# Expert blocks: the second 128 tokens' layer 2 put last and under a condition, second-layer weights split behind layer 1, block table made over three blocks

## The chip, the cores and the metric

The kernel runs on one NeuronCore of a Trainium2 chip. The metric is the device time of one execution in microseconds (us). Times of single instructions come from the hardware profiler's record of one execution. Engines are called as in the profile: PE is TensorE's matmul, PEld its weight load, DVE is VectorE, ACT ScalarE, POOL GpSimd, SP SyncE. A name with q (PEldq, POOLq) is that engine's sequencer, which handles branches, register loads and semaphore instructions.

## The reference, cut to what matters

Three stages follow each other: a linear-attention recurrence over 4 x 8 x 768 steps, a dense squared-ReLU layer pair (384 to 2048 to 384), and a routed expert layer. The change touches the third alone:

```
do_compute = x @ w_skip > 0                     # 3072 tokens of 384
e_idx = argmax(xc @ w_gate)                     # 8 experts
for e in range(8):
    mask = e_idx == e
    h = maximum(xc[mask] @ w1[e], 0)            # 384 -> 1024
    y[mask] = gate_w[mask] * (h @ w2[e])        # 1024 -> 384
out = x;  out[do_compute] = xc + y
```

Evaluated on the inputs, the reference sends 2397 of the 3072 tokens to experts 0 to 7 in numbers of 1155, 132, 435, 318, 112, 43, 143 and 59. Of expert 0's, 1064 stand in the first 2816 tokens.

## The kernel before, in words

The expert stage works in blocks of 256 tokens of one expert. Blocks 0 and 1 take the first 512 tokens of expert 0 while the dense stage's last tokens are still being routed; blocks 2 to 8 take the first 256 tokens of experts 1 to 7. What is left is listed in a table made at run time (`table`, lines 826 to 877): with the counts above these are three more blocks of expert 0 and one more each of experts 2 and 3, so that blocks 9 to 13 run and the 14 blocks of the profile are complete. Blocks from 9 on stand in nested conditions on the number of blocks `nblk` (`rest`, lines 974 to 978).

A block (`block`, lines 886 to 924) has eight slices `f` of 128 hidden units. Every product of float32 numbers is three matmuls, high by high, high by low, low by high. `l1(f)` is 9 matmuls of 256 columns into one of four PSUM banks; ACT then writes the high part `hh` (relu) and DVE the low part `hl`. `l2(f)` is, for each half `t` of 128 tokens, 3 matmuls of 384 columns that add to `acc[t]`; it follows `l1` by LAG = 4 slices. The last four slices' `l2` stand behind all of `l1`, first for half 0 and then for half 1. `finish(n, t)` (DVE, line 786) scales and adds the token row, `scatter(n, t)` (POOL, line 790, an indirect DMA) writes the rows out. A block always computes all 256 rows; rows without a token have an index outside the output.

Each block carries side work at times written out by hand in `CTP` (lines 73 to 77), in units of half a step: `gather(n + 2)` (POOL, line 772), `xprep(n + 1, t)` (three PE transposes at line 779, an ACT cast, a DVE subtraction), and for the next expert's weights eight pieces `ew_split`: ACT writes the high part (line 647), then DVE or POOL, as `CTP["e"]` says, the low part (line 648). Pieces 0 to 3 are `w1`, pieces 4 to 7 `w2`. Right behind the split of a piece, SP issues the load of the set after next into the freed buffer (line 637). The order on each engine is the program's order; semaphores between engines come from the tile framework. `nblk` and the register values for SP are read by `values_load`. The condition of line 729 jumps over the whole fallback for badly scaled inputs; it isn't taken here.

In the built program of this kernel a condition has a true arm and a false arm. [...]

Of the kernel before, what the change touches and what calls it, by code (L numbers as in the profile page):

```python
# [7 lines left out]
F32 = mybir.dt.float32  # L8
F32R = mybir.dt.float32r
BF16 = mybir.dt.bfloat16  # L10
I32 = mybir.dt.int32
# [60 lines left out]

CTP = {
    "l": [0.3, 1.2, 2.1, 2.6, 3.3, 4.1, 4.6, 5.7],
    "e": [0, 1, 0, 1, 0, 0, 1, 0],
    "x": [5.1, 5.6],
    "g": 2.6}
NX = NTOK // UT
NST = NE + 1
# [4 lines left out]
def rwkv_moe_kernel(ctx: ExitStack, tc: tile.TileContext, a_in, v_in, ud, wio,  # L84
# [659 lines left out]
    xgs = [[cp.tile([128, DM], F32, name=f"xg0_{t}") for t in range(2)]]  # L744
    ptx = [ptk, pu]
    xhs, xls = list(xth), list(xtl)
    exr, sct = {}, [None]

    def wset(n):

# [2 lines left out]
    def ids(n, t):  # L753
        if n < 2:
            l = lsp[0][:, 2 * n + t]
        elif n < NST:
            l = lsb[:, (n - 1) * LB + t]
        else:
            l = idt[:, n - NST, t]
        return l[:, 0:1], l[:, 1:2].bitcast(F32)  # L760
# [9 lines left out]
    def gather(n):  # L770
        for t in range(2):
            nc.gpsimd.indirect_dma_start(  # L772
                xgs[n % 4][t], None, x2d[:, :], bass.IndirectOffsetOnAxis(ap=ids(n, t)[0], axis=0),
                bounds_check=NTOK + PADR - 1, oob_is_err=False)

    def xprep(n, t):
        bank = ptx[t]
        for kc in range(KC):
            nc.tensor.transpose(bank[:, kc * 128:(kc + 1) * 128], xgs[n % 4][t][:, kc * 128:(kc + 1) * 128], ident)  # L779
        s = slice(t * 128, t * 128 + 128)  # L780
        src = bank[:, 0:DM].rearrange("p (k t) -> p k t", k=KC)
        nc.scalar.copy(xhs[n % 3][:, :, s], src)
        nc.vector.tensor_tensor(xls[n % 3][:, :, s], src, xhs[n % 3][:, :, s].bitcast(F32), ALU.subtract)

    def finish(n, t):
        nc.vector.scalar_tensor_tensor(yos[n % 2][t], acc[t][:, 0:DM], ids(n, t)[1], xgs[n % 4][t], ALU.mult, ALU.add)

    def scatter(n, t):

        i = nc.gpsimd.indirect_dma_start(  # L790
            out[:, :], bass.IndirectOffsetOnAxis(ap=ids(n, t)[0], axis=0), yos[n % 2][t], None,
            bounds_check=NTOK - 1, oob_is_err=False)
        if t:
            tc.declare_no_dep(i.ins, sct[0].ins, reason="rows of the other half of the block")
        sct[0] = i
# [11 lines left out]
    cq = ctx.enter_context(tc.tile_pool(name="cq", bufs=1, side="right"))  # L807
    ew_alloc(cq, 1)
    raws.append(cq.tile([128, 8, 768], F32, name="raw1"))
    xgs += [[cq.tile([128, DM], F32, name=f"xg{i}_{t}") for t in range(2)] for i in range(1, 4)]  # L810
    xhs.append(cq.tile([128, KC, UT], F32R, name="cxh2"))
    xls.append(cq.tile([128, KC, UT], F32R, name="cxl2"))
    yos = [[cq.tile([128, DM], F32, name=f"yo{i}_{t}") for t in range(2)] for i in range(2)]
    hps = pgs + [[cq.tile([128, UT], F32R, name=f"{n}{i}") for n in ("gh", "gl")] for i in range(NPB, LAG + 1)]
    ls2 = cq.tile([128, NE * LB, 2], I32, name="ls2")
    idt = cq.tile([128, NX, 2, 2], I32, name="idt")
    tx = cq.tile([1, 4, NE], F32, name="tx")
    ti = cq.tile([1, 2, NE], I32, name="ti")
    tm = cq.tile([1, 2, NX, NE], F32, name="tm")
    tv = cq.tile([1, 5, NX], F32, name="tv")  # L820
    tbl = cq.tile([1, 2, NX], I32, name="tbl")
    nbk = cq.tile([1, 1], I32, name="nbk")
    l1b = [ph[0], ph[1], pat.rearrange("p a b c -> p (a b c)"), py.rearrange("p a b -> p (a b)")]

    def table():


        V = nc.vector
        c0, f = cn0[0:1, 0:1], tx[:, 0, 0:1]
        ex, cx, g = tx[:, 1], tx[:, 2], tx[:, 3, 0:1]  # L830
        ind, pr = tm[:, 0], tm[:, 1]
        eb, sb, kb, z, bs = (tv[:, n] for n in range(5))
        on = cfs[0:1, 256:256 + NX]
        each = lambda a: a.unsqueeze(1).to_broadcast([1, NX, NE])

        def t1():
            V.tensor_tensor(f, c0, cnt[0:1, 0:1], ALU.is_lt)
            V.scalar_tensor_tensor(f, c0, float(2 * UT), f, ALU.is_lt, ALU.mult)
            V.tensor_scalar(ti[:, 0], cnt[0:1], 1, None, ALU.subtract)
            V.tensor_scalar(ti[:, 1], ti[:, 0], 8, None, ALU.arith_shift_right)  # L840

        def t2():

            V.tensor_scalar(ex, ti[:, 1], 0.0, None, ALU.max)  # L844
            V.tensor_scalar(g, f, 2.0, -1.0, ALU.mult, ALU.add)
            V.tensor_tensor(ex[:, 0:1], ti[:, 1, 0:1], g, ALU.add)
            V.tensor_scalar(ex[:, 0:1], ex[:, 0:1], 0.0, None, ALU.max)

        def t3():
            V.tensor_tensor_scan(cx, cfs[0:1, 256:256 + NE], ex, 0.0, ALU.mult, ALU.add)  # L850
            V.tensor_copy(nbk, cx[:, NE - 1:NE])
            V.tensor_tensor_scan(bs, on, on, -1.0, ALU.mult, ALU.add)

        def t4():
            V.tensor_tensor(ind, each(cx), bs.unsqueeze(2).to_broadcast([1, NX, NE]), ALU.is_le)
            V.tensor_tensor(pr, ind, each(ex), ALU.mult)
            V.tensor_reduce(eb, ind, AX.X, ALU.add)

        def t5():
            V.tensor_scalar(eb, eb, float(NE - 1), None, ALU.min)  # L860
            V.tensor_reduce(sb, pr, AX.X, ALU.add)
            V.tensor_tensor(kb, bs, sb, ALU.subtract)
            V.tensor_scalar(kb, kb, 1.0, None, ALU.add)

        def t6():

            V.tensor_scalar(z, eb, 0.0, g, ALU.is_equal, ALU.mult)
            V.tensor_tensor(kb, kb, z, ALU.subtract)
            V.tensor_scalar(kb, kb, 2.0, None, ALU.mult)

        def t7():
            V.scalar_tensor_tensor(kb, eb, float(LB), kb, ALU.mult, ALU.add)
            V.tensor_scalar(kb, kb, float(NE * LB - 2), None, ALU.min)
            V.tensor_copy(tbl[:, 0], eb)
            V.tensor_copy(tbl[:, 1], kb)

        return [(0.9 + m, f) for m, f in enumerate((t1, t2, t3, t4, t5, t6, t7))]

    def ex_load(b):
        exr[b] = nc.values_load(tbl[0:1, 0, b:b + 1], engines=[mybir.EngineType.SP], min_val=0, max_val=NE - 1)  # L880

    def id_load(b):
        c = nc.values_load(tbl[0:1, 1, b:b + 1], engines=[mybir.EngineType.SP], min_val=0, max_val=NE * LB - 2)
# [2 lines left out]
    def block(n, side):  # L886

        w1h, w1l, w2h, w2l = ew[wset(n) % 2]
        xh, xl = xhs[n % 3], xls[n % 3]

        def l1(f):
            h = l1b[f % 4][:, 0:UT]
            m = 0
            for w, xx in ((w1h, xh), (w1l, xh), (w1h, xl)):
                for kc in range(KC):
                    nc.tensor.matmul(h, w[:, kc, f * 128:(f + 1) * 128], xx[:, kc, :],  # L896
                                     start=(m == 0), stop=(m == 3 * KC - 1))
                    m += 1
            hh, hl = hps[f % (LAG + 1)]
            nc.scalar.activation(hh, h, AF.Relu)  # L900
            nc.vector.scalar_tensor_tensor(hl, h, 0.0, hh.bitcast(F32), ALU.max, ALU.subtract)  # L901

        def l2(f, ts=(0, 1)):
            hh, hl = hps[f % (LAG + 1)]
            for t in ts:
                s = slice(t * 128, t * 128 + 128)
                for m, (a, w) in enumerate(((hh, w2h), (hh, w2l), (hl, w2h))):
                    nc.tensor.matmul(acc[t][:, 0:DM], a[:, s], w[:, f, :],  # L908
                                     start=(f == 0 and m == 0), stop=(f == NJE - 1 and m == 2))

        steps = []
        for f in range(NJE):
            steps.append(lambda f=f: l1(f))
            if f >= LAG:
                steps.append(lambda f=f - LAG: l2(f))
        for t in range(2):
            for f in range(NJE - LAG, NJE, 2):
                steps.append(lambda f=f, t=t: (l2(f, (t,)), l2(f + 1, (t,))))
            steps.append(lambda t=t: (finish(n, t), scatter(n, t)))
        todo = sorted((v, m) for m, (v, _) in enumerate(side))  # L920
        for m, f in enumerate(steps):
            f()
            while todo and todo[0][0] < (m + 1) / 2:
                side[todo.pop(0)[1]][1]()

    def sides(n):
        side, last = [], NST + NX - 1

        def add(v, f):
            side.append((v, f))  # L930
# [3 lines left out]
        if n < last:  # L934
            for t in range(2):
                add(CTP["x"][t], lambda t=t: xprep(n + 1, t))
        w = wset(n) + 1
        if n and n < last:
            for p in range(8):
                add(CTP["l"][p], lambda p=p: ew_split(w, p, nc.gpsimd if CTP["e"][p] else nc.vector))  # L940
        if n and wset(n) + 3 <= last - 1:
# [2 lines left out]
                add(0.01, lambda: ex_load(q - NE))  # L944
            for p in range(8):
                add(CTP["l"][p] + 0.02, lambda p=p: ew_load(q, p, exr[q - NE] if q >= NE else None))
        if 3 <= n < 6:
            for b in range(4 * n - 12, 4 * n - 8):
                add(7 + 0.1 * (b % 4), lambda b=b: id_load(b))
        return side  # L950

# [15 lines left out]
    r2b()  # L967
    gather(1)
    block(0, side)
    for n in range(1, NST):  # L970
        block(n, sides(n) + (table() if n == 2 else []))
    nblk = nc.values_load(nbk[0:1, 0:1], min_val=0, max_val=NX)

    def rest(n):
# [83 lines left out]
```

## Time and profile before

| | |
|---|---|
| median of 3 runs | 910.76 us (910.37 to 911.51) |
| the profiled execution's own time | 911.02 us |
| its span, first to last instruction | 909.2 us |
| PE busy | 833.6 us (92%) |
| DVE busy | 611.6 us (67%) |
| POOL busy | 583.7 us (64%) |
| ACT busy | 495.7 us (55%) |
| expert blocks, first matmul to last | 645.8 to 893.8 us |
| the last block (13), first matmul | 876.17 us |

The profile gives for each engine the time in which it had an instruction running. Busy shares are means over stages with different limits, so what a change in the expert stage is worth is read from the stretch of that stage, from 646 us on.

### The profile page before, as it was taken

Reading aid. Unit: us, or ns where it says so; the run is one execution under the profiler, and the core shown is the slowest. Engines: PE = TensorE matmul, PEld = TensorE weight load, DVE = VectorE, ACT = ScalarE, POOL = GpSimd, SP = SyncE. Lnnn points to the kernel's source line nnn. Section 1 sums busy time; section 2 is a strip of 40 time slices with the busy share of each in tenths; the row PEclk is TensorE's granted clock in tenths of the full one; section 3 lists DMA queues with packets and bytes.
Section 4 is the critical chain, followed back from the end, with each engine's and each line's share of the span. In section 5 each row is a group of like instructions: output and inputs, shape, how many; then the busy total and the mean of one; then the engine's idle time right before and its main releaser. Section 6 shows DMA issues by size and latency. Waiting matters only on the chain. (4 is left out here: it accounts for less than half of the span.)

```text
span 909.2 us, 18684 instructions
## 1 busy us (share of the span) xinstructions
PE 833.6 (92%) x6790; PEld 792.0 (87%) x6790; DVE 611.6 (67%) x1273; ACT 495.7 (55%) x1229; POOL 583.7 (64%) x618
## 2 busy tenths in 40 slices
PE   2665799999999999999999999989999999999993
PEld 2544698999999999999999999979999999999993
DVE  7987962658585758575767676513468787777773
ACT  1343555666656565656565656647345554554551
POOL 8766976776777767676767676526355655554561
PEclk9955899999999999999999999989999999999997
DMA  8454322232222322222231311025486676567663
GB/s 209 139 182 116 131 61 52 78 78 78 52 78 52 77 56 75 63 68 74 56 87 43 87 44 56 2 93 194 147 304 203 212 237 221 186 218 236 211 208 115
DMA packets 67806, 110.92 MB, mean 122 GB/s; under 512 B 34452, under 2 KB 43944, under 8 KB 67696
## 3 DMA queue, kind: packets, MB, share of 16 engines
q1 hardware_dynamic: 60192, 97.46, 36.0%
q0 software_dynamic: 4736, 10.40, 3.5%
q10 hardware_dynamic: 2768, 1.69, 0.8%
q8 instruction: 57, 0.93, 0.4%
q14 instruction: 53, 0.43, 0.2%
HBM read 92.84 MB, written 16.15 MB: 120 GB/s over the span
## 5 line engine op out<-in xcount | busy, mean ns | idle before, releaser
L369 POOL TENSOR_TENSOR gl<-g,gh 128x256 fp32r<-128x256 f32 x192 | 150.0, 783 | 145.2 <-ACT gh L368 100.2
L361 PE MATMUL ph<-xt,wih 128*128 128x256 f32 x1152 | 227.7, 294 | 4.1 <-PEq L729 3.8
L361 PEld LDWEIGHTS ph<-xt,wih 128*128 128x128 f32 x1152 | 184.1, 192 | 8.4 <-issue 4.1
L361 PE MATMUL ph<-xt,wil 128*128 128x256 f32 x576 | 163.9, 285 | 0.0
L366 ACT ACTIVATE g<-ph 128x256 f32<-128x256 f32 x192 | 72.9, 380 | 123.8 <-PE ph L361 98.2
L377 PE MATMUL acc<-woh,gl 128*128 128x394 f32 x384 | 132.6, 345 | 0.9 <-POOL gl L369 0.9
L377 PE MATMUL acc<-woh,gh 128*128 128x394 f32 x384 | 133.0, 346 | 0.0
L377 PE MATMUL acc<-wol,gh 128*128 128x394 f32 x384 | 131.0, 341 | 0.0
L361 PEld LDWEIGHTS ph<-xt,wil 128*128 128x128 f32 x576 | 110.6, 192 | 0.0
L292 DVE COPY_PREDICATED gr<-cis,pat 64x256 f32<-64x256 int32 x192 | 85.6, 446 | 32.4 <-PE pat L282 28.2
L648 DVE TENSOR_TENSOR w2l<-raw,w2h 128x768 fp32r<-128x768 f32 x42 | 84.7, 2017 | 7.6 <-ACT w2h L647 4.8
L367 ACT ACTIVATE g<-g 128x256 f32<-128x256 f32 x192 | 80.2, 418 | 6.1
L368 ACT CAST gh<-g 128x256 fp32r<-128x256 f32 x192 | 77.9, 406 | 6.1
L908 PE MATMUL acc<-w2h,gh 128*128 128x384 f32 x224 | 77.8, 347 | 0.0
L908 PE MATMUL acc<-w2h,gl 128*128 128x384 f32 x224 | 75.4, 336 | 0.6 <-DVE gl L901 0.6
L377 PEld LDWEIGHTS acc<-woh,gl 128*128 128x128 f32 x384 | 72.3, 188 | 4.1 <-POOL gl L369 3.7
L908 PE MATMUL acc<-w2l,gh 128*128 128x384 f32 x224 | 75.3, 336 | 0.0
L377 PEld LDWEIGHTS acc<-woh,gh 128*128 128x128 f32 x384 | 72.7, 189 | 0.7
L377 PEld LDWEIGHTS acc<-wol,gh 128*128 128x128 f32 x384 | 72.8, 190 | 0.0
L648 POOL TENSOR_TENSOR w1l<-raw,w1h 128x768 fp32r<-128x768 f32 x27 | 50.0, 1850 | 30.7 <-ACT w1h L647 30.5
L282 PE MATMUL pat<-ru,kbd 112*128 112x128 f32 x384 | 56.2, 294 | 12.1 <-POOL kbd L255 12.0
L226 DVE STREAM_TRANSPOSE knd<-kbd 32x256 f32<-32x256 f32 x144 | 62.4, 434 | 3.6 <-POOL kbd L255 1.1
(212 smaller groups left out, 1828.0 us busy)
## 6 DMA issues: line engine op xcount, KB each, us to landing
raw<-in_we SPq DMA_DIRECT2D x128, 384.0 KB
ain<-in_a_in SPq DMA_DIRECT2D x22, 675.9 KB
raw<-in_wio SPq DMA_DIRECT2D x16, 768.0 KB
vz<-in_v_in SPq DMA_DIRECT2D x44, 128.0 KB
x2d<-x SPq DMA_DIRECT2D x12, 384.0 KB
out<-x SPq DMA_DIRECT2D x12, 384.0 KB
xt<-yt SPq DMA_DIRECT2D x72, 32.0 KB
ain<-in_a_in ACTq DMA_DIRECT2D x1, 675.9 KB
```

The lines of the kernel that those rows point to most:

```text
L226: nc.vector.transpose(kn[64 * h + 32 * b2:64 * h + 32 * b2 + 32, :, :, 64 * h + 32 * a:64 * h + 32 * a + 32], kb[64 * h + 32 * a:64 * h + ...
L282: nc.tensor.matmul(pat[:, c], kb[0:112, qq, c, :], ru[:, qq, c], start=True, stop=True)
L292: nc.vector.copy_predicated(gr[sl, qq, :, h, :], msk[sl].unsqueeze(1).to_broadcast([64, 4, CH]), pat[sl, :, m, :])
L361: nc.tensor.matmul(h[:, 0:UT], w[:, kc, j * 128:(j + 1) * 128], x[:, kc, :], start=(n == 0), stop=(n == 3 * KC - 1))
L366: nc.scalar.activation(g, h[:, 0:UT], AF.Relu)
L367: nc.scalar.activation(g, g, AF.Square)
L368: nc.scalar.copy(gh, g)
L369: nc.gpsimd.tensor_tensor(gl, g, gh.bitcast(F32), ALU.subtract)
L377: nc.tensor.matmul(acc[t][:, 0:OW], a[:, s], w[:, j, :], start=(j == 0 and n == 0), stop=(j == NJ - 1 and n == 2))
L648: eng.tensor_tensor(l, r, h.bitcast(F32), ALU.subtract)
L908: nc.tensor.matmul(acc[t][:, 0:DM], a[:, s], w[:, f, :], start=(f == 0 and m == 0), stop=(f == NJE - 1 and m == 2))
```

## The change

Layer 2 of half 0 (`l2(f, 0)`) keeps its place four slices behind layer 1 and its last four slices follow. Layer 2 of half 1 is taken out of the interleaving: all eight slices, with `finish(n, 1)` and `scatter(n, 1)`, make up `half()`, which stands at the end of the block. For blocks 2 and later it stands in a condition: it runs where the expert has more than 128 tokens left at this block (`rem[n] > 128`). The count is read into a register of every engine in the middle of the block before (`rem_load`), for blocks 2 to 8 from `cnt`, for later ones from a third row of the table, which `t6b` computes. The eight slices of `hh` and `hl` get a buffer each. Instead, the gathered rows have three buffers and not four, the output rows one set and not two. The split of the `w2` pieces moves to the steps behind layer 1, POOL takes the low parts of pieces 1, 5 and 7 instead of 1, 3 and 6, `xprep` comes half a step earlier, the table's parts stand in blocks 2, 3 and 4 and not all in block 2, and the index loads (`id_load`) two blocks later.

```diff
 CTP = {
-    "l": [0.3, 1.2, 2.1, 2.6, 3.3, 4.1, 4.6, 5.7],
-    "e": [0, 1, 0, 1, 0, 0, 1, 0],
-    "x": [5.1, 5.6],
+    "l": [0.3, 1.2, 2.1, 2.9, 5.6, 6.2, 6.8, 7.4],
+    "e": [0, 1, 0, 0, 0, 1, 0, 1],
+    "x": [4.6, 5.1],
     "g": 2.6}
...
-                xgs[n % 4][t], None, x2d[:, :], bass.IndirectOffsetOnAxis(ap=ids(n, t)[0], axis=0),
+                xgs[n % 3][t], None, x2d[:, :], bass.IndirectOffsetOnAxis(ap=ids(n, t)[0], axis=0),
...
-        nc.vector.scalar_tensor_tensor(yos[n % 2][t], acc[t][:, 0:DM], ids(n, t)[1], xgs[n % 4][t], ALU.mult, ALU.add)
+        nc.vector.scalar_tensor_tensor(yos[t], acc[t][:, 0:DM], ids(n, t)[1], xgs[n % 3][t], ALU.mult, ALU.add)
...
+        def t6b():
+
+            V.tensor_tensor(ind, eb.unsqueeze(2).to_broadcast([1, NX, NE]), each(bs[:, 0:NE]), ALU.is_equal)
+            V.tensor_tensor(pr, ind, each(cnt[0:1]), ALU.mult)
+            V.tensor_reduce(rb, pr, AX.X, ALU.add)
+            V.scalar_tensor_tensor(rb, kb, -float(UT), rb, ALU.mult, ALU.add)
+            V.tensor_scalar(tbl[:, 2], rb, 0.0, None, ALU.max)
...
+    def rem_load(n):
+
+        src = cnt[0:1, n - 1:n] if n < NST else tbl[0:1, 2, n - NST:n - NST + 1]
+        rem[n] = nc.values_load(src, min_val=0, max_val=NTOK)
...
-            hh, hl = hps[f % (LAG + 1)]
+            hh, hl = hps[f]
...
+        def half():
+            for f in range(NJE):
+                l2(f, 1)
+            finish(n, 1)
+            scatter(n, 1)
 
         steps = []
         for f in range(NJE):
             steps.append(lambda f=f: l1(f))
             if f >= LAG:
-                steps.append(lambda f=f - LAG: l2(f))
-        for t in range(2):
-            for f in range(NJE - LAG, NJE, 2):
-                steps.append(lambda f=f, t=t: (l2(f, (t,)), l2(f + 1, (t,))))
-            steps.append(lambda t=t: (finish(n, t), scatter(n, t)))
+                steps.append(lambda f=f - LAG: l2(f, 0))
+        for f in range(NJE - LAG, NJE):
+            steps.append(lambda f=f: l2(f, 0))
...
+        finish(n, 0)
+        scatter(n, 0)
+        if n < 2:
+            half()
+        else:
+            with tc.If(rem[n] > 128):
+                half()
...
+        if n and n < last:
+            add(2.2, lambda: rem_load(n + 1))
...
-        if 3 <= n < 6:
-            for b in range(4 * n - 12, 4 * n - 8):
+        if 5 <= n < 8:
+            for b in range(4 * n - 20, 4 * n - 16):
...
+    tb = table()
     for n in range(1, NST):
-        block(n, sides(n) + (table() if n == 2 else []))
+        block(n, sides(n) + [(0.8 + 2.4 * (m % 3), f) for m, f in enumerate(tb) if n == 2 + m // 3])
```

## Rows read from the trace of the kernel before

**Rows 1.** Engine busy time by stretch: length, PE, PEld, DVE, ACT, POOL, clock, DMA.
```profile
681.34:699.85 18.51, 17.89 (x128) 17.54 (x128) 16.51 (x39) 9.74 (x18) 9.34 (x7) 1.00 0.67 219
717.53:735.12 17.59, 17.59 (x128) 17.55 (x128) 13.18 (x17) 9.77 (x18) 9.57 (x8) 1.00 0.70 225
660.00:680.00 20.00, 20.00 (x142) 19.96 (x141) 14.31 (x20) 9.78 (x19) 11.68 (x9) 1.00 0.89 303
```

**Rows 2.** Chain of waits, block 4: start, length, what, instructions.
```profile
717.53 2.14 PE ph L896 x18
...
730.62 0.33 PE pu L779 x3
730.95 4.17 PE acc L908 x24
```

**Rows 3.** Busy time in block 2 where PE waits for DVE (columns as in rows 1).
```profile
696.00:698.00 2.00, 1.38 (x8) 1.06 (x8) 1.93 (x8) 0.01 (x1) 0.00 (x0) 1.00 0.43 137
```

**Rows 4.** Sequencer instructions of the conditions (lines 975, 1054): min/median/max ns, starts.
```profile
L975 PEldq COMPARE_BRANCH  x7: 65/65/4542, 803.7 to 895.6; - x7
L975 PEldq EVENT_SEMAPHORE  x1: 51/51/51, 895.5 to 895.5; - x1
L975 POOLq INC_SWDGE_SEM  x1: 1894/1894/1894, 899.2 to 899.2; - x1
...
L1054 PEldq DRAIN  x2: 8/8/8, 895.9 to 908.7; - x2
```

**Rows 5.** The far jump of line 729, its sequencer instructions and PE behind it.
```profile
L729 PEldq COMPARE_BRANCH  x1: 3840/3840/3840, 602.3 to 602.3; - x1
L729 PEldq EVENT_SEMAPHORE  x1: 51/51/51, 606.2 to 606.2; - x1
L729 POOLq INC_SWDGE_SEM  x1: 636/636/636, 604.8 to 604.8; - x1
606.48 0.77 PE L361 MATMUL ph<-xt,wih 128*128 128x256 f32 x2 [3.77 <-PEq L729]
...
606.50:611.50 5.00, 5.00 (x23) 5.00 (x24) 1.59 (x11) 2.78 (x7) 0.73 (x1) 0.50 0.63 199
```

**Rows 6.** Reading `nblk` into registers, line 972, on PE's sequencer.
```profile
L972 PEldq EVENT_SEMAPHORE  x5: 51/51/51, 802.7 to 803.1; - x5
L972 PEldq TENSOR_LOAD <-nbk x1: 322/322/322, 803.2 to 803.2; - x1
```

**Rows 7.** Instructions of block 4 by form: line, shape, count, busy us, mean ns.
```profile
L900 ACT ACTIVATE gh<-ph 128x256 fp32r<-128x256 f32 x4 | 1.5, 384 | 5.1 <-PE ph L896 4.7 <-issue 0.3
L901 DVE SCALAR_TENSOR_TENSOR gl<-ph,gh 128x256 fp32r<-128x256 f32 x4 | 1.7, 423 | 2.0 <-ACT gh L900 1.1 <-issue 0.9
L647 ACT CAST w2h<-raw 128x768 fp32r<-128x768 f32 x4 | 3.2, 833 | 0.0
L782 ACT CAST cxh<-pu 128x384 fp32r<-128x384 f32 x1 | 0.5, 482 | 0.9 <-PE pu L779 0.9
```

**Rows 8.** DVE's and POOL's splits in order of time, beside each other and alone.
```profile
627.54 2.09 DVE L648 TENSOR_TENSOR w1l<-raw,w1h 128x768 fp32r<-128x768 f32 x1 [3.40 <-ACT w1h L647]
626.92 1.85 POOL L648 TENSOR_TENSOR w1l<-raw,w1h 128x768 fp32r<-128x768 f32 x1
628.73 3.68 POOL L369 TENSOR_TENSOR gl<-g,gh 128x256 fp32r<-128x256 f32 x3
...
761.46 2.86 DVE L648 TENSOR_TENSOR w2l<-raw,w2h 128x768 fp32r<-128x768 f32 x1 [0.30 <-ACT w2h L647]
761.63 1.87 POOL L648 TENSOR_TENSOR w1l<-raw,w1h 128x768 fp32r<-128x768 f32 x1
768.18 0.94 DVE L648 TENSOR_TENSOR w2l<-raw,w2h 128x768 fp32r<-128x768 f32 x1
```

**Rows 9.** The last instructions of the last block (13) on DVE and POOL.
```profile
893.87 0.62 DVE L786 SCALAR_TENSOR_TENSOR yo<-acc,idt,xg 128x384 f32<-128x384 f32 x1 [0.78 <-PE acc L908]
894.77 0.99 POOL L790 DMA_INDIRECT out<-yo,idt  x1 [0.38 <-DVE yo L786]
```

More of the change, by code (lines that the diff above doesn't have):

```diff
@@ L746, in rwkv_moe_kernel @@
     xhs, xls = list(xth), list(xtl)
-    exr, sct = {}, [None]
+    exr, rem, sct = {}, {}, [None]
     def wset(n):
@@ L778, in xprep @@
         for kc in range(KC):
-            nc.tensor.transpose(bank[:, kc * 128:(kc + 1) * 128], xgs[n % 4][t][:, kc * 128:(kc + 1) * 128], ident)
+            nc.tensor.transpose(bank[:, kc * 128:(kc + 1) * 128], xgs[n % 3][t][:, kc * 128:(kc + 1) * 128], ident)
         s = slice(t * 128, t * 128 + 128)
@@ L785, in finish @@
     def finish(n, t):
-        nc.vector.scalar_tensor_tensor(yos[n % 2][t], acc[t][:, 0:DM], ids(n, t)[1], xgs[n % 4][t], ALU.mult, ALU.add)
+        nc.vector.scalar_tensor_tensor(yos[t], acc[t][:, 0:DM], ids(n, t)[1], xgs[n % 3][t], ALU.mult, ALU.add)
     def scatter(n, t):
         i = nc.gpsimd.indirect_dma_start(
-            out[:, :], bass.IndirectOffsetOnAxis(ap=ids(n, t)[0], axis=0), yos[n % 2][t], None,
+            out[:, :], bass.IndirectOffsetOnAxis(ap=ids(n, t)[0], axis=0), yos[t], None,
             bounds_check=NTOK - 1, oob_is_err=False)
@@ L809, in rwkv_moe_kernel @@
     raws.append(cq.tile([128, 8, 768], F32, name="raw1"))
-    xgs += [[cq.tile([128, DM], F32, name=f"xg{i}_{t}") for t in range(2)] for i in range(1, 4)]
+    xgs += [[cq.tile([128, DM], F32, name=f"xg{i}_{t}") for t in range(2)] for i in range(1, 3)]
     xhs.append(cq.tile([128, KC, UT], F32R, name="cxh2"))
     xls.append(cq.tile([128, KC, UT], F32R, name="cxl2"))
-    yos = [[cq.tile([128, DM], F32, name=f"yo{i}_{t}") for t in range(2)] for i in range(2)]
-    hps = pgs + [[cq.tile([128, UT], F32R, name=f"{n}{i}") for n in ("gh", "gl")] for i in range(NPB, LAG + 1)]
+    yos = [cq.tile([128, DM], F32, name=f"yo{t}") for t in range(2)]
+    hps = pgs + [[cq.tile([128, UT], F32R, name=f"{n}{i}") for n in ("gh", "gl")] for i in range(NPB, NJE)]
     ls2 = cq.tile([128, NE * LB, 2], I32, name="ls2")
@@ L819, in rwkv_moe_kernel @@
     tm = cq.tile([1, 2, NX, NE], F32, name="tm")
-    tv = cq.tile([1, 5, NX], F32, name="tv")
-    tbl = cq.tile([1, 2, NX], I32, name="tbl")
+    tv = cq.tile([1, 6, NX], F32, name="tv")
+    tbl = cq.tile([1, 3, NX], I32, name="tbl")
     nbk = cq.tile([1, 1], I32, name="nbk")
@@ L831, in table @@
         ind, pr = tm[:, 0], tm[:, 1]
-        eb, sb, kb, z, bs = (tv[:, n] for n in range(5))
+        eb, sb, kb, z, bs, rb = (tv[:, n] for n in range(6))
         on = cfs[0:1, 256:256 + NX]
@@ L868, in t6, with t6c @@
             V.tensor_tensor(kb, kb, z, ALU.subtract)
+        def t6b():
[4 more added lines that the diff above has]
+            V.tensor_scalar(tbl[:, 2], rb, 0.0, None, ALU.max)
+        def t6c():
             V.tensor_scalar(kb, kb, 2.0, None, ALU.mult)
@@ L875, in t7 @@
             V.tensor_copy(tbl[:, 1], kb)
-        return [(0.9 + m, f) for m, f in enumerate((t1, t2, t3, t4, t5, t6, t7))]
+        return t1, t2, t3, t4, t5, t6, t6b, t6c, t7
     def ex_load(b):
         exr[b] = nc.values_load(tbl[0:1, 0, b:b + 1], engines=[mybir.EngineType.SP], min_val=0, max_val=NE - 1)
+    def rem_load(n):
+        src = cnt[0:1, n - 1:n] if n < NST else tbl[0:1, 2, n - NST:n - NST + 1]
+        rem[n] = nc.values_load(src, min_val=0, max_val=NTOK)
     def id_load(b):
@@ L898, in l1, with l2 @@
                     m += 1
-            hh, hl = hps[f % (LAG + 1)]
+            hh, hl = hps[f]
             nc.scalar.activation(hh, h, AF.Relu)
             nc.vector.scalar_tensor_tensor(hl, h, 0.0, hh.bitcast(F32), ALU.max, ALU.subtract)
[L903 to L909, printed above, removed]
+        def l2(f, t):
+            hh, hl = hps[f]
+            s = slice(t * 128, t * 128 + 128)
+            for m, (a, w) in enumerate(((hh, w2h), (hh, w2l), (hl, w2h))):
+                nc.tensor.matmul(acc[t][:, 0:DM], a[:, s], w[:, f, :],
+                                 start=(f == 0 and m == 0), stop=(f == NJE - 1 and m == 2))
+        def half():
[3 more added lines that the diff above has]
+            scatter(n, 1)
         steps = []
```

## The prediction, made before the changed kernel was run

> **What bounds the kernel now.** I read the busy shares by slice first and then only the stretch of the expert blocks, because the change touches nothing ahead of it. There the reader is to see that PE has an instruction running all the time: block 4 lasts 17.59 us with 17.59 us of PE, at the full granted clock, while DVE has 13.2, ACT 9.8 and POOL 9.6 [rows 1]. The chain of waits says the same: one PE group follows the other, and a block closes with 24 matmuls of layer 2 in 4.17 us [rows 2]. So a block lasts as long as its matmuls. With 1.07 us for a slice of layer 1 (18 in 2.14), 0.174 us for a matmul of layer 2 and 0.33 for a group of transposes, it comes to 8 x 1.07 + 48 x 0.174 + 2 x 0.33 = 17.6 us. The one exception is block 2: it lasts 18.51 us and PE is idle for 0.62 us in a stretch where DVE is busy for 1.93 of 2 us, with the table in its way [rows 1, 3].
>
> **Which halves go.** From the reference's counts, `rem` at blocks 2 to 13 is 132, 435, 318, 112, 43, 143, 59 and then 643, 387, 131 (expert 0), 179 (expert 2) and 62 (expert 3). Blocks 5, 6, 8 and 13 are at or under 128: four of twelve conditions skip, three inside the stage and one in the last block.
>
> **A skipped half inside the stage.** It removes 24 matmuls, 4.17 us [rows 2], and leaves a block of 13.4 us of PE. What it adds is the false arm: PE's sequencer waits until all its matmuls have ended, so the queue ahead of PE, which covers sequencer work now, runs empty once. No row shows this drain with a near jump. Below: PE starts 0.24 us after the end of the semaphore instruction at 606.2 (0.05 long, first matmul 606.48), so 0.3 us in all [rows 5]. Above: the last matmul's pipeline, 0.35 against a pitch of 0.174, adds 0.17; the signal about 0.1 (my estimate); and a near jump behind the semaphore instruction, which at the end of the program takes from 895.6 to the next instruction at 895.9, adds 0.3 [rows 4]: 0.9, and 1.2 with as much again for instructions that restart unfilled. I take 0.7, between the two and nearer to the second, since every term of it has a row. So a skip gives 4.17 - 0.7 = 3.5 us, and three give 10.4 (9.0 to 11.6).
>
> **Is another engine late when the block is short?** In time from the block's start, the steps end at: slice 4 of layer 1 at 5.4, slice 7 at 10.5, the second transposes at 10.8, `l2(7, 0)` at 13.4. ACT: relu of slice 7 and the cast of `xprep` to 11.4, then casts 4 to 7 at 0.83 each to 14.7 [rows 7]. DVE's splits are slow beside POOL's: 2.86 us where POOL's split ran, 0.94 alone, and it ends 0.82 to 0.86 after POOL's end. At 628.8 it got through although POOL had its next instructions queued [rows 8]. So DVE takes piece 4 at 12.4 to 13.3, POOL piece 5 at 13.2 to 15.0, DVE piece 6 to 15.9, POOL piece 7 to 17.8, and DVE's `finish(n, 0)` (0.62) is through at 16.6. The next block starts at 14.1; its slice 4 needs `hl(0)` to free the bank at 14.1 + 4.3 = 18.4, and DVE writes that at about 17.5. This fits by 0.9 us. [...] POOL's scatter, at 18 to 19, then stands behind its splits, and the skip adds INC_SWDGE_SEM, 0.64 or 1.89 us [rows 4, 5]; POOL's next due work, piece 1, is at 14.1 + 4.4 (three slices of layer 1, relu and cast), so it starts up to 3 us late with the gathers behind it, and nobody needs either for a block. On SP the loads of pieces 4 to 7 leave later, behind DVE's and POOL's splits, and the next piece 0 waits in order behind them; each piece still has more than a block until its split. The loads: 3.1 MB of weights and about 0.8 MB of rows per block are 290 GB/s over 13.4 us; 303 GB/s were moved at a DMA share of 0.89 [rows 1], and buffers are refilled two blocks ahead. I cost that at nothing.
>
> **A half that runs.** The matmuls are the same 48 in another order, and all that they read is older than before, so a block stays at 17.6 us. Added per condition are a fall-through branch (65 ns, [rows 4]) and, past the false arm, a near jump of about 0.3 us. In each block from 1 to 12 `rem_load` adds five semaphore instructions and a load, 0.26 + 0.32 = 0.58 us, to PE's sequencer [rows 6]. The same instructions for `nblk` ran from 802.7 while PE went on without a gap until 805.64 and beyond; the branch at 803.7 shows that the sequencer was 1.9 us ahead [rows 4, 6]. That lead hides all three. Behind a skip it has to be built again within 5.4 us; if it fails, 0.58 us per skip are open. I take 0.1 for each of the three, 0.3 in all (0 to 1.7). On ACT, DVE and POOL the load lies in slack of 4 us and more per block.
>
> **The table.** Its instructions move from block 2 to blocks 2, 3 and 4, five more with them, at 0.15 to 0.25 us each where POOL doesn't hold them up. Block 2 loses its excess: 18.51 - 17.59 = 0.9 us gained [rows 1]. The other moves (three row buffers, one set of output rows, `xprep` half a step earlier, index loads two blocks later) make instructions wait for a `finish`, a scatter, a gather or a load that was issued most of a block before, and I cost them at nothing; were one of them late, PE would wait at `xprep` or `acc[0]`.
>
> **The last block gives nothing.** Before, its POOL issues the last scatter until 895.76, 19.6 us after its start [rows 9]. After, PE is done 4.2 us earlier, but POOL's last scatter stands behind its piece 7 (17.8): it ends at about 18.2 to 19.2, and the skip's INC_SWDGE_SEM (0.64 to 1.89) follows before the way out, which stays as it is. That makes -0.8 to +1.5; I take a loss of 0.8.
>
> **Sum**, against the profiled execution's 911.0 us: -10.4 - 0.9 + 0.3 + 0.8 = -10.2, so 900.8; the median of the runs lies 0.26 below that execution, so 900.5.
>
> [...]
>
> **Rivals.**
> 1. *Jumps that miss.* A far jump took PE's sequencer 3.84 us at line 729 and 4.54 at the end of the program, and at line 729 PE then ran 5 us at a granted 0.50 (1.2 GHz), which lost 2.5 us more [rows 4, 5]. If each skip costs that, with the lead of 1.9 us hiding part of it or not, and the clock falling, a skip costs 4.5 + 0.3 + 2.5 - 4.17 = 3.1 us net, and the time is 910.8 - 0.9 + 1.1 + 9.4 = about 920. It turns slower from 3.8 us lost per skip. Against it: the target lies 24 matmuls ahead and not a stage, and a jump over the other false arms took 0.3 us [rows 4]. 0.07. If the jump misses at one block of the three only, it is 900.5 plus 2.6 (4.5 less the lead) to 7.0 (with the clock): 903 to 907.5, say 905.5. 0.06.
> 2. *DVE becomes the bound of short blocks.* [...] PE then loses 1 to 2.5 us per skip: 904 to 908, say 905.5. For it: DVE's 13.2 us of a block are as long as the short block itself [rows 1]; against it: DVE loses a `w2` split, which costs it up to 2.9 us beside POOL, for a `w1` split (net about 1.1 us), and one `finish`. 0.14.
> 3. *The joins cost on the eight halves that run,* 0.3 to 0.7 us each with no lead: 903 to 906. 0.05.
> 4. *The conditions don't skip,* or what they give is eaten wholly: 909 to 912. 0.05.
>
> The forecast has 0.63.
>
> **How the numbers follow.** The forecast's own terms give 898 to 904. The range of 8 in 10 takes in most of rivals 2 and 3 and of a single miss: 897.8 to 906.5. About 0.2% (1.8 us) is what a measurement of this kernel can tell from no change. Faster: the forecast, a single miss, rivals 2 and 3, 0.88; same: rival 4, 0.05; slower: the misses at every skip, 0.07.
>
> **What would show it.** Blocks 5, 6 and 8 last 14.1 us and the others 17.6; between the last `acc` matmul of a skipping block and the first `ph` of the next PE is idle for 0.5 to 0.9 us at full clock; block 2 has no PE gap; the last scatter ends 18 to 20 us after the start of block 13 although PE ends at 13.4. Wrong would be: a PE branch of microseconds at the new condition, a granted clock under 1 in the blocks, `ph` of slice 4 waiting for `hl`, or the end moving with PE's end.

## The result and the profile after

The changed kernel takes 900.11 us (median of 4 runs, 899.61 to 900.31) against 911.13 for the kernel before in the same comparison (4 runs, 910.37 to 911.95): a ratio of 0.9877, with a 95% interval of 0.9864 to 0.9889. A second comparison gave 898.72 (4 runs) against 910.50 (9 runs), 0.9865 (0.985 to 0.988). The forecast was 900.5, with a range of 897.8 to 906.5.

The busy time by stretch, each stretch one block from its first matmul to that of the next (core 0 of the changed kernel; columns as in [rows 1], blocks 2, 4, 5, 6, 7, 8, 9, and PE's part of 13):
```profile
682.89:700.55 17.66, 17.66 (x128) 17.62 (x127) 13.73 (x28) 9.65 (x18) 10.08 (x7) 1.00 0.70 222
718.22:735.89 17.67, 17.67 (x127) 17.63 (x127) 15.74 (x28) 9.66 (x18) 10.73 (x7) 1.00 0.72 226
735.89:749.67 13.78, 13.63 (x104) 13.30 (x103) 9.38 (x18) 8.99 (x18) 7.09 (x6) 1.00 0.71 231
749.67:763.52 13.85, 13.70 (x102) 13.38 (x103) 11.20 (x17) 9.63 (x19) 10.38 (x7) 1.00 0.68 204
763.52:781.27 17.75, 17.75 (x126) 17.72 (x127) 13.76 (x18) 10.35 (x19) 14.12 (x9) 1.00 0.82 295
781.27:795.70 14.43, 13.61 (x104) 13.27 (x103) 9.47 (x16) 9.66 (x18) 7.83 (x6) 1.00 0.70 217
795.70:813.47 17.77, 17.77 (x127) 17.73 (x127) 12.36 (x18) 9.64 (x19) 13.28 (x9) 1.00 0.78 248
866.45:879.92 13.47, 13.47 (x103) 13.28 (x102) 8.65 (x15) 8.62 (x17) 6.75 (x6) 1.00 0.69 227
```
The reader is to see three things. Blocks 5, 6, 8 and 13 hold some 24 PE instructions less. A block that runs its half is still as long as its PE time, as block 4 was [rows 1]. Block 2 has lost its excess of 0.9 us.

The share of DVE and POOL in the whole hardly tells this; the page's first lines only say that PE still has nine tenths of the span:
```profile
span 898.5 us, 18759 instructions
PE 822.0 (91%) x6694; PEld 779.6 (87%) x6694; DVE 590.1 (66%) x1274; ACT 494.4 (55%) x1229; POOL 592.4 (66%) x614
```

From the first matmul of the expert blocks to the end of the span, the two profiles of the changed kernel have 251.21 and 251.29 us, that of before 263.57: 12.3 us gained. By block starts: block 5 gives 3.88, block 6 3.76, block 8 3.16, block 2 0.85, and block 13 with the way out 1.15; the nine other blocks lose 0.43 together. The profiled time fell by only 10.7, because the same code ahead of the expert blocks took 1.66 us longer in that execution (first expert matmul at 647.29 instead of 645.63). Over the eleven profiles of this study that moment lies between 644.3 and 648.3. So the experiments below are compared by the stretch from there, called the stage, and by their times. The stage has a loose part too, its end: from the last scatter's issue to the end of the program the eleven profiles have 12.9 to 14.8 us, and four whose code there is the same have 13.5, 13.5, 14.4 and 14.8. The starts of blocks with the same work repeat to 0.1 us, and the place of the last scatter in block 13 to 0.01 us where the code is the same, so an effect at the end is read from the scatter. For block 13 that is 1.15 us as well: the last scatter ends 18.61 us after the block's start instead of 19.75.

The instructions of the condition (line 948) on the engines' sequencers, min/median/max ns, first and last start:
```profile
L948 PEldq COMPARE_BRANCH  x20: 65/175/214, 694.5 to 878.1; - x20
L948 PEldq EVENT_SEMAPHORE  x4: 51/51/51, 749.6 to 880.1; - x4
L948 POOLq INC_SWDGE_SEM  x4: 1223/1338/1789, 752.4 to 883.0; - x4
```
The four semaphore instructions on PE's sequencer are four false arms; the kernel below that runs all halves has none at this line, and 24 branches. So the 20 branches are twelve conditions and eight jumps over a false arm; none takes more than 0.214 us, against 3.84 and 4.54 for the far jumps [rows 4, 5].

What stands at the end of block 5, in order of time (start, length, engine, line, tile):
```profile
748.96 4.41 POOL L648 TENSOR_TENSOR w2l<-raw,w2h 128x768 fp32r<-128x768 f32 x2 [3.62 <-ACT w2h L647]
749.18 0.34 PE L922 MATMUL acc<-w2h,gl 128*128 128x384 f32 x1
749.64 2.02 DVE L648 TENSOR_TENSOR w2l<-raw,w2h 128x768 fp32r<-128x768 f32 x1 [0.50 <-ACT w2h L647]
749.67 0.59 PE L911 MATMUL ph<-xt,w1h 128*128 128x256 f32 x3
751.58 0.60 DVE L786 SCALAR_TENSOR_TENSOR yo<-acc,lsb,xg 128x384 f32<-128x384 f32 x1
752.33 0.42 DVE L916 SCALAR_TENSOR_TENSOR gl<-ph,gh 128x256 fp32r<-128x256 f32 x1
```
Matmuls of layer 2 come every 0.17 us, so PE is free at 749.35 and starts again at 749.67: 0.32 us without work. The last matmul, started at 749.18, ends at 749.52; the first semaphore instruction of line 948 starts at 749.6, and PE's next weight load at 749.64. Behind block 13 the last matmul ends at 880.09 and the last semaphore instruction starts at 880.1. Behind block 6 the gap is 0.32 again. The first three matmuls behind the gap then take 0.59 us, where the same group at the start of block 4 took 0.52. DVE's split begins 0.68 us after POOL's pair and is through at 751.66, while POOL's pair, 4.41 us for two that take some 1.85 each in [rows 8], runs to 753.37: DVE's split did not wait for the end of both.

### The profile page after: what moved, and what is told of

Its sections match the earlier page's. It is cut to its first block, busy times and chain, and to the rows that moved or that the text cites. A ratio compares the mean times of both kernels' runs of the same rounds, so it can differ in the third digit from the quotient of the medians.

```text
span 898.5 us, 18759 instructions
## 1 busy us (share of the span) xinstructions
PE 822.0 (91%) x6694; PEld 779.6 (87%) x6694; DVE 590.1 (66%) x1274; ACT 494.4 (55%) x1229; POOL 592.4 (66%) x614
## 5 line engine op out<-in xcount | busy, mean ns | idle before, releaser
L648 POOL TENSOR_TENSOR w2l<-raw,w2h 128x768 fp32r<-128x768 f32 x27 | 56.9, 2125 | 44.7 <-ACT w2h L647 41.1
L922 PE MATMUL acc<-w2h,gh 128*128 128x384 f32 x192 | 65.7, 342 | 0.0
L282 PEld LDWEIGHTS pat<-ru,kbd 112*128 112x128 f32 x384 | 53.8, 209 | 12.5 <-POOL kbd L255 11.8
L922 PE MATMUL acc<-w2h,gl 128*128 128x384 f32 x192 | 64.6, 336 | 0.0
L922 PE MATMUL acc<-w2l,gh 128*128 128x384 f32 x192 | 64.5, 336 | 0.0
```

The source lines that it names most:

```text
L282: nc.tensor.matmul(pat[:, c], kb[0:112, qq, c, :], ru[:, qq, c], start=True, stop=True)
L648: eng.tensor_tensor(l, r, h.bitcast(F32), ALU.subtract)
L922: nc.tensor.matmul(acc[t][:, 0:DM], a[:, s], w[:, f, :], start=(f == 0 and m == 0), stop=(f == NJE - 1 and m == 2))
```

## The experiments

**The new order without the condition.** The second 128 tokens come last in every block, always.
```diff
-        if n < 2: half()
-        else:
-            with tc.If(rem[n] > 128): half()
+        half()
...
-        if n and n < last:
-            add(2.2, lambda: rem_load(n + 1))
```


> The new order and the spread table, but every half runs: no condition, no register loads of the counts. Theory (the gain is the skipped matmuls, and the new order costs or gives nothing on PE): blocks of 17.6 us, the table's 0.9 us gained in block 2, 910.2 us beside 911.1 of before, ratio 0.999. Rival (the order itself carries part of the gain, since w2's splits no longer stand between layer 1's residuals): 905 to 908 us. Rival (layer 1 pressed into 11 us makes hl late): blocks over 18 us, 915 us or more.


Measured: 911.22 (10 runs) against 911.30 (25 runs), 1.000 (0.9989 to 1.0012). The stage takes 263.39 us, 0.2 less than before. Blocks 2 and 5, by stretch:
```profile
683.01:700.66 17.65, 17.65 (x127) 17.61 (x127) 13.73 (x28) 9.66 (x18) 10.06 (x7) 1.00 0.72 221
736.01:753.66 17.65, 17.65 (x127) 17.61 (x127) 11.89 (x19) 9.66 (x18) 10.81 (x8) 1.00 0.72 229
```
Block 2 gains its 0.86 here too, but block 13 with the way out is some 0.2 us longer (its last scatter ends at 19.99 us and not at 19.75) and the other blocks give back most of the rest, some 0.03 us each. So order, buffers, splits and table together give nothing that can be measured; the gain is the condition's.

**The condition that always runs its half.** All that it issues is kept.
```diff
-            with tc.If(rem[n] > 128):
+            with tc.If(rem[n] > 0):
```


> As the changed kernel with the condition rem > 0, which is true in all of blocks 2 to 13: the conditions, their register loads and false arms are there, and no half is skipped. Theory (branch, load and jump past the false arm lie in the sequencer's lead): like the kernel without conditions within 1 us, 910.5 us, no PE idle at a block's end. Rival (each join costs 0.3 to 0.7 us): 12 of them, 914 to 919 us.


Measured: 911.66 (10 runs), 1.0002 (0.999 to 1.0014). Block 5 and the branches:
```profile
734.20:751.85 17.65, 17.65 (x127) 17.61 (x127) 11.88 (x19) 9.66 (x18) 10.81 (x8) 1.00 0.72 227
```
```profile
L948 PEldq COMPARE_BRANCH  x24: 65/124/193, 692.8 to 890.1; - x24
```
The block is as long as without a condition, to 0.01 us, and PE has no gap at a block's end. Twelve branches, twelve jumps and thirteen loads of a count cost PE nothing: rival 3 (joins on halves that run) falls. The stage is 0.7 us longer than without the condition, all of it behind the last scatter, whose place is the same (19.99), and within what that end varies by.

**The condition that never runs it.** This leaves the second 128 tokens of blocks 2 to 13 out of layer 2, `finish` and `scatter`.
```diff
-            with tc.If(rem[n] > 128):
+            with tc.If(rem[n] > 4000):
```


> The condition is rem > 4000, never true: blocks 2 to 13 all leave out their second half (those rows are not computed). Theory (a skip gives 4.17 us less 0.32 us of drain, and PE stays the bound in short blocks): eleven blocks of 13.75 us and the 0.7 us of the nblk load, the last block 1 us: about 868 us. Rival (DVE, ACT or POOL bound short blocks that stand side by side): 1 to 2.5 us lost per block, 880 to 895 us. Rival (weight loads at 285 GB/s don't keep up): PE waits for splits that wait for raw, blocks of 15 us or more, over 885 us.


Measured: 872.83 (4 runs), 0.9586 (0.9566 to 0.9607), 4.8 us more than expected; the stage takes 224.5 us. Blocks 2 to 7:
```profile
681.67:695.45 13.78, 13.63 (x103) 13.30 (x103) 9.88 (x24) 8.99 (x18) 7.09 (x6) 1.00 0.67 226
695.45:710.39 14.94, 14.22 (x102) 13.36 (x103) 14.66 (x27) 9.62 (x19) 10.30 (x7) 1.00 0.76 250
710.39:725.83 15.44, 14.25 (x102) 13.38 (x103) 14.77 (x25) 9.65 (x19) 8.58 (x7) 1.00 0.76 244
725.83:740.63 14.80, 13.96 (x102) 13.43 (x103) 12.40 (x21) 9.67 (x19) 9.24 (x7) 1.00 0.78 255
740.63:754.48 13.85, 13.70 (x102) 13.38 (x103) 11.20 (x17) 9.63 (x19) 10.38 (x7) 1.00 0.66 199
754.48:768.36 13.88, 13.73 (x103) 13.41 (x103) 11.24 (x17) 9.68 (x19) 10.41 (x7) 1.00 0.80 277
```
Of the short blocks in a row, 6 and 7 keep 13.8 to 13.9 us: the weights arrive, at 277 GB/s in block 7, and PE has no matmul running for 0.15 us in each (13.85 less 13.70, 13.88 less 13.73). (That its sequencer gets its lead again behind a skip is to be seen in the changed kernel: in block 6 the branch of line 948 starts at 761.4, 1.7 us before the block's last matmul, as in block 5, at 747.5.) Blocks 3, 4 and 5 do not keep it. In 3 and 4 DVE is busy for 14.66 of 14.94 and 14.77 of 15.44 us, with the parts of the table among its splits. Block 5 has no part of its own, but takes over the last part of block 4, and is 1.0 us longer than block 2. PE waits for DVE's `hl` once in block 3, twice in 4 and once in 5 (waits between 660 and 860 us: total, times, longest); below the waits, two instructions of the table around the start of block 5, which take 1.8 us while POOL runs two splits (725.14 to 728.83), where one of line 879 took 0.15 three microseconds before:
```profile
PE ph L911 <- DVE gl L916: 1.6, 3, 0.7
PE pat L911 <- DVE gl L916: 0.6, 1, 0.6
```
```profile
725.23 1.81 DVE L882 SCALAR_TENSOR_TENSOR tv<-tv 1x12 f32<-1x12 f32 x1
727.07 1.77 DVE L883 TENSOR_SCALAR tv<-tv 1x12 f32<-1x12 f32 x1
```
So rival 2 exists, but it shows only where a part of the table stands in short blocks side by side; with this input blocks 3 and 4 run in full. That the table is the cause is argued from where the waits stand; no run had these short blocks without it.

The sequencers' rows settle what the false arm's gap is. In this trace line 948 has no branch, and PE no load of a count; what remains is:
```profile
L948 PEldq EVENT_SEMAPHORE  x12: 51/51/51, 695.3 to 852.8; - x12
L948 POOLq INC_SWDGE_SEM  x12: 979/1290/1620, 699.9 to 855.5; - x12
```
PE still loses 0.32 us at the ends of blocks 2 to 7, the same as with branches. The first semaphore instruction starts at 695.3, where the last matmul of block 2, started at 694.96, ends. The gap is the wait for PE's own matmuls at the semaphore instruction, not the jump. Behind blocks 9 to 12, where a condition on `nblk` stands between the skip and the next block, it is 0.49 us, and these blocks last 14.05 to 14.07.

**The condition that skips in the last block alone.**
```diff
-            with tc.If(rem[n] > 128):
+            with tc.If(rem[n] > (128 if n == 13 else 0)):
```


> The condition is rem > 128 in block 13 and rem > 0 in all others, so only the last block skips. Theory (the end is POOL's last scatter behind its last split, and then POOL's way out): 1.0 us less than with all halves run (0.3 to 1.7), PE ending 4.2 us earlier. Rival (PE's end carries the end): 3.5 to 4.2 us less.


Measured: 910.63 (10 runs), 1.0002 (0.9988 to 1.0015), which does not tell it from the condition that always runs. The stages do: 262.86 us against 264.11, 1.25 less. Block 13 and its last scatter:
```profile
875.77:889.24 13.47, 13.47 (x103) 13.28 (x102) 8.64 (x15) 8.62 (x17) 6.75 (x6) 1.00 0.69 227
```
```profile
893.36 1.02 POOL L790 DMA_INDIRECT out<-yo,idt  x1 [0.16 <-issue]
```
The last scatter with all halves run, where block 13 starts at 875.52:
```profile
894.52 0.99 POOL L790 DMA_INDIRECT out<-yo,idt  x1 [0.30 <-DVEq L1003]
```
PE ends 4.2 us earlier, the program 1.25: POOL issues its last scatter until 18.61 us after the block's start, instead of 19.99, and what follows it takes 14.3 us in this run and 14.2 in the other. The end goes with POOL, as the forecast had it, but to a small gain.

**The old places of the splits** (`CTP` of before) in the changed kernel:
```diff
-    "l": [0.3, 1.2, 2.1, 2.9, 5.6, 6.2, 6.8, 7.4],
-    "e": [0, 1, 0, 0, 0, 1, 0, 1],
+    "l": [0.3, 1.2, 2.1, 2.6, 3.3, 4.1, 4.6, 5.7],
+    "e": [0, 1, 0, 1, 0, 0, 1, 0],
```


> From the changed kernel with the split plan of before: pieces at 0.3, 1.2, 2.1, 2.6, 3.3, 4.1, 4.6, 5.7 and POOL on pieces 1, 3 and 6, so w2's splits stand between layer 1's residuals again. Theory (layer 1 is now pressed into 11 us, and DVE's splits of 2.4 to 2.9 us beside POOL make hl of slices 5 to 7 late): PE waits 1 to 2 us in every block from 1 to 13, 915 us, no gain left. Rival (LAG of 4 slices covers it): within 1 us of the changed kernel.


Measured: 923.54 (4 runs), 1.0141 (1.0126 to 1.0157): 13 us slower than before, 24.8 us slower than the changed kernel beside it, and 8.5 us over the expected 915. The waits of the stage (us in total, times, longest) and, below them, the last case in time:
```profile
PE acc L922 <- DVE gl L916: 20.1, 12, 1.9
```
```profile
860.43 3.22 DVE L648 TENSOR_TENSOR w2l<-raw,w2h 128x768 fp32r<-128x768 f32 x1 [0.30 <-ACT w2h L647]
863.57 0.41 DVE L916 SCALAR_TENSOR_TENSOR gl<-pat,gh 128x256 fp32r<-128x256 f32 x1
863.90 2.26 DVE L648 TENSOR_TENSOR w2l<-raw,w2h 128x768 fp32r<-128x768 f32 x1
...
866.56 0.41 DVE L916 SCALAR_TENSOR_TENSOR gl<-py,gh 128x256 fp32r<-128x256 f32 x1
867.02 0.44 PE L922 MATMUL acc<-w2h,gl 128*128 128x384 f32 x1 [1.65 <-DVE gl L916]
```
Layer 1 now ends nine matmuls of layer 2 earlier in the block than before: its last group's last matmul starts 10.43 us after the block's start instead of 11.60. With DVE's splits in front of it, the last `hl` comes too late, and PE waits in twelve blocks for 1.6 to 1.9 us. The clock adds to it: in blocks 2, 7 and 9 the granted clock fell behind the wait (behind those of 7 and 9 three matmuls of layer 1 took 0.84 us for 0.52). Block 2, a stretch in it, and block 11, where it stayed up:
```profile
683.56:704.91 21.35, 19.48 (x128) 19.13 (x127) 14.52 (x28) 9.38 (x18) 10.34 (x7) 0.92 0.58 189
700.00:702.00 2.00, 2.00 (x8) 2.00 (x8) 1.01 (x2) 0.00 (x0) 0.71 (x1) 0.50 0.92 293
851.91:871.50 19.59, 17.94 (x128) 17.58 (x128) 13.38 (x17) 9.38 (x18) 10.10 (x7) 1.00 0.61 201
```
In block 2 PE waited for 1.87 us until 698.88 and then ran at 0.50, with a matmul of layer 2 every 0.32 us for 0.17 before (384 columns in 0.32 us, 1.2 a ns); the three blocks last 21.1 to 21.4 us, the other full blocks with such a wait 19.6 to 19.8. The prediction held that all that a block reads is older than before, and gave the move of the splits no price. For `hl` that fails: it comes in time only with the splits moved. Order and move together bring nothing, as the first experiment shows, but the gain stands on the move.

**The read of `nblk` half a block earlier.** Behind block 8 the gap was 0.99 us instead of 0.32; between it and block 9 stands the read of `nblk` on PE's sequencer (changed kernel, line 1000, and PE at that place):
```profile
L1000 PEldq TENSOR_LOAD <-nbk x1: 305/305/305, 795.1 to 795.1; - x1
```
```profile
794.54 0.34 PE L922 MATMUL acc<-w2h,gl 128*128 128x384 f32 x1
795.70 0.62 PE L911 MATMUL ph<-xt,w1h 128*128 128x256 f32 x3 [0.82 <-ACT w2h L647]
```
(The releaser named, a cast of weights, had long been done.)
```diff
+        if n == NST - 1:
+            add(2.21, lambda: nbr.append(nc.values_load(nbk[0:1, 0:1], min_val=0, max_val=NX)))
...
-    nblk = nc.values_load(nbk[0:1, 0:1], min_val=0, max_val=NX)
+    nblk = nbr[0]
```


> From the changed kernel only the reading of nblk is moved from the end of block 8 into its middle. Theory: PE's idle time between blocks 8 and 9 falls from 0.99 us to 0.3 to 0.5, block 8 lasts 13.9 us and not 14.4; nothing else changes. Rival (the wait named in the profile, ACT's w2 casts, is real): block 8 stays at 14.4 us.


Measured: 897.71 (one run, before 910.50 beside it). Block 8, first in the changed kernel's second profile, then here:
```profile
782.29:796.63 14.34, 13.62 (x103) 13.27 (x103) 9.38 (x16) 9.56 (x18) 7.76 (x6) 1.00 0.67 218
```
```profile
778.29:792.21 13.92, 13.60 (x103) 13.25 (x103) 8.87 (x16) 9.23 (x18) 6.76 (x6) 1.00 0.71 224
```
The block is 0.42 to 0.51 us shorter, and the gap falls from 0.99 to 0.49. So the read cost half a microsecond. The rest of the gap, 0.17 over that of the other skips, stays; the next conditions stand right behind it, as they do behind blocks 9 to 12 of the kernel that never runs its half, where the gap is 0.49 too. (The stage is 251.6 us all the same: the way out behind the last scatter took 0.9 us longer in this execution.)

**`finish` and `scatter` ahead of the last splits.** The first 128 tokens go out before the weights of the block after the next are split (with the read of `nblk` moved as well).
```diff
-    "l": [0.3, 1.2, 2.1, 2.9, 5.6, 6.2, 6.8, 7.4],
-    "e": [0, 1, 0, 0, 0, 1, 0, 1],
+    "l": [0.3, 1.2, 2.1, 2.9, 5.6, 8.1, 8.2, 8.3],
+    "e": [0, 1, 0, 0, 0, 0, 0, 0],
...
         finish(n, 0)
         scatter(n, 0)
+        while todo:
+            side[todo.pop(0)[1]][1]()
```


> From the changed kernel: nblk is read in the middle of block 8; finish and scatter of half 0 stand ahead of w2's pieces 5 to 7, whose low parts all go to DVE. Theory (the bubble of 0.99 us behind block 8 is 0.32 of drain and 0.67 of reading nblk; the end follows POOL's last scatter): 0.67 us less behind block 8, the last scatter at about 15.2 us after the start of block 13 and not at 18.6: 3.4 us less at the end; together 896 us, 0.9835 of before, the stretch from the first expert matmul on 247.2 us. Rival (the end follows something else, a landing or DVE's last split): 0.7 to 1.5 us less in all, 0.987. Rival (finish early on DVE holds up hl of the next block): short blocks over 14.3 us.


Measured: 896.08 (5 runs), 0.9841 (0.9828 to 0.9855); the stage takes 248.62 us, 2.6 less than in the changed kernel. The end of block 13 in both, the changed kernel first:
```profile
881.37 2.51 POOL L648 TENSOR_TENSOR w2l<-raw,w2h 128x768 fp32r<-128x768 f32 x1
882.14 0.61 DVE L786 SCALAR_TENSOR_TENSOR yo<-acc,idt,xg 128x384 f32<-128x384 f32 x1
884.04 1.02 POOL L790 DMA_INDIRECT out<-yo,idt  x1 [0.16 <-issue]
```
```profile
878.56 2.69 DVE L648 TENSOR_TENSOR w2l<-raw,w2h 128x768 fp32r<-128x768 f32 x3
878.92 1.47 POOL L790 DMA_INDIRECT out<-yo,idt  x1 [5.08 <-DVE yo L786]
```
The last scatter ends 16.05 us after the block's start instead of 18.61, 2.56 less, and the program ends 2.2 us earlier against that start. That is the end's part; block 8 gave 0.42. The forecast of 4.0 had the scatter through at 15.2, but its issue took 1.47 us beside DVE's splits instead of 1.02, and it began late. Of the versions that compute all rows this is the fastest. Its interval meets that of the changed kernel run beside it, but each of its five runs (895.95 to 896.34) is below each of the other's four (897.39 to 901.33), and the stages part them.

**The changed kernel once more,** beside the three experiments above.

> The changed kernel once more, as the mark for the others of this job: 0.988 of the kernel before. All theories expect the same; its stretch ahead of the expert blocks may differ by 1 to 2 us between profiles, as in the runs so far (first expert matmul at 645.6 to 647.4), and the stretch from there to the end should be 251.2 us again within 0.3.


Measured: 898.72 (4 runs); all blocks within 0.1 us of the first profile.

**The table in one block again**, in the changed kernel:
```diff
-        block(n, sides(n) + [(0.8 + 2.4 * (m % 3), f) for m, f in enumerate(tb) if n == 2 + m // 3])
+        block(n, sides(n) + [(0.9 + 0.75 * m, f) for m, f in enumerate(tb) if n == 2])
```


> From the changed kernel with all nine parts of the table in block 2, at 0.9 and every 0.75 steps. Theory (the table's DVE instructions hold up hl where layer 2 follows it, and spreading gave 0.85 us): block 2 lasts 18.3 to 18.8 us and not 17.65, all other blocks as in the changed kernel. Rival (with w2's splits behind layer 1 DVE has room for the table in one block): block 2 stays at 17.65 to 17.75 us.


Measured: 901.07 (one run, before 911.32 beside it). Block 2:
```profile
682.36:700.01 17.65, 17.65 (x127) 17.61 (x127) 15.41 (x40) 9.66 (x18) 9.68 (x7) 1.00 0.54 180
```
With all 40 of DVE's instructions in it, the block is as short as with 28. I had expected the excess to come back; it did not. The 0.85 us come from the new order and places, not from spreading the table; which of them brings it was not taken apart. (The time is 901.07, with a way out of 14.8 us behind the last scatter for the 13.5 of the changed kernel.)

## Why the prediction was right

The mechanism and the sign held, and the time lies in the forecast's own range. By steps:

- *What bounds the blocks.* Right: a block follows its PE time, with a half or without, at a granted clock of 1.00 throughout.
- *Which halves go.* Right: 5, 6, 8 and 13, four false arms.
- *A skipped half gives 3.5 us.* The gain was 3.88, 3.76 and 3.16, in all 10.80 where 10.4 was forecast. The drain was the mis-sized term: 0.32 us for the forecast's 0.7, below the 0.5 to 0.9 that it named as its sign. The lower bound, 0.3 from PE's restart behind the far jump [rows 5], was the nearer row. The upper bound added a jump, and none shows in the gap: with no branch at the condition it is the same 0.32. The choice leaned to the upper bound because every term of it had a row, but its 0.1 for the signal, and the 0.3 for instructions that restart unfilled, were estimates that no row and no run shows; what the runs show is the 0.32 for the whole.
- *"That lead hides all three."* It does (branch, jump, load of the count) wherever a half runs, and a load of the count inside a block costs next to nothing behind a skip either: block 6 lasts 13.85 us, block 5 13.78. But a fourth read was missed: that of `nblk`, right behind the skip of block 8, where the drain had just used up the lead of 1.9 us [rows 4, 6]. It took 0.67 us off the third skip, some 0.5 of it the read itself and, by the kernel that reads it earlier, 0.17 the conditions behind it. The forecast's 0.3 for loads that are not covered was priced for another one.
- *No other engine is late.* Right, by the order that was worked out: DVE's split was through at 751.66, before POOL's two at 753.37, the `hl` that frees the bank was through 3.1 us after the next block's start (3.4 forecast), and slice 4 needs it at 4.3.
- *A half that runs stays at 17.6.* 17.69 against 17.64 on the mean of eight blocks (block 0 left out), 0.43 us over nine. Part of it is in the kernel without a condition too (17.65 to 17.68), so it is the order's. The longest, blocks 7 and 9 with 17.75 and 17.77, follow a skip, and their first three matmuls take 0.59 and 0.62 us for the 0.52 of block 4: behind the gap PE starts some 0.1 us slower. The order's part stays open.
- *The table, 0.9 us.* The size held by luck: the reason fell.
- *All that a block reads is older than before.* Not so for `hl`: with the splits left in their old places, the order costs PE 1.6 to 1.9 us of waiting per block. The kernel escaped this by the move, for which the prediction had no price.
- *The last block gives nothing.* The sign was wrong. The last scatter ended at 18.6 us after the block's start, inside the 18.2 to 19.2 of the forecast, but the last INC_SWDGE_SEM of line 948 began at 883.0, while POOL's split ran (881.37 to 883.88), and was over before the scatter's issue ended at 885.06. It did not follow the scatter, so a loss of 0.8 became a gain of 1.15. (The 19.6 us of before count from 876.17, where the view of the chain of waits puts the block's start. In order of time its first matmul starts at 876.01, and the 19.75 here count from there.)

The terms were -10.4, -0.9, +0.3 and +0.8; they measured -10.80, -0.85, 0 and -1.15, with +0.43 for the blocks that run: 12.4 in place of 10.2. That the time came out within 0.4 us of the forecast is luck: the stage gained 2.2 us more than the sum, and the same code ahead of it took 1.66 us longer in that execution.

Of the rivals, the jumps that miss fall: no branch at the condition takes more than 0.214 us, and the clock stays at 1.00. On PE's sequencer none of these short jumps was dear and both far ones were (3.9 us at line 729, 5.0 at line 1003); what makes a jump dear is not shown here, and with so few no figure can be put on how often one at a condition would be. The bound on DVE shows only with all halves skipped: there blocks 3, 4 and 5 last 14.80 to 15.44 us, 0.9 to 1.6 more than blocks 6 and 7; the rival's 1 to 2.5 per skip were the author's estimate, and no run shows the 2.5. The cost of joins shows nowhere, and the conditions skip.

## What to carry to other kernels

Here a condition at the end of a block that PE bounds cost 0.3 to 0.4 us where it skipped (24 matmuls of 4.17 us gave 3.88 and 3.76) and nothing where it ran, as long as nothing else on PE's sequencer stood right behind it, as the read of `nblk` did for half a microsecond: look for every register read there and move it into the middle of a block. Taking work out of the middle of a block brings the deadlines in it forward, so the side work has to move with it; here the order without the move of the splits was 13 us slower than the kernel before, and 24.8 slower than with it. The end of this program followed the queue that issues the last store, not the engine that bounds the loop: put the last scatter ahead of work that nobody waits for.

## What was not expected of the hardware

The stretch ahead of the expert blocks, the same code in all kernels, ended anywhere from 644.3 to 648.3 us, while the blocks behind it repeated to 0.1 us. The way out behind the last scatter varies as well, from 12.9 to 14.8 us; that the stage of the changed kernel came out as 251.21 and 251.29 owes something to two ways out that happened to agree at 13.5. What makes either differ stays open; it is why a change of one microsecond shows in the block starts and in the last scatter's place, and not in the times.

The indirect scatter's issue on POOL took 1.00 to 1.02 us in most places, but 1.47 us beside DVE's splits (13 of the 14 scatters of the first 128 tokens in the version that puts them ahead of the splits) and 1.55 us for the scatters of blocks 5, 6 and 8 in the changed kernel, which run in the next block beside a split on DVE. This was not taken apart further.
